# Fewer, larger transfers for the transposed keys of an attention kernel, and a list schedule that counts the issue time of the SP queue

## The chip, the cores and the metric

The kernel runs on one core of a Trainium2 chip. It is written in a Python kernel language that gives each engine its own instruction stream: PE (TensorE: matrix products and transposes), DVE (VectorE), ACT (ScalarE), POOL (GpSimd) and SP (SyncE, whose queue issues nearly all DMA transfers). The engines run at the same time and each works through its own stream in order; they wait for one another through semaphores. The metric is the device time of one launch in microseconds (us), lower is better.

## The reference

The program computes a recurrent attention over 768 steps for 4 batches of 8 heads (head dimension 40), and then a mixture of eight experts on its output.

```python
for t in range(S):                       # S=768; r,k,v,w,a,b are (4,8,768,40)
    y[:, :, t] = np.einsum('bhd,bhde->bhe', rt, state)
    Sa = np.einsum('bhde,bhe->bhd', state, at)
    state_decay = state * wt[:, :, None, :] - np.einsum('bhd,bhe->bhde', Sa, bt)
    state = state_decay + np.einsum('bhd,bhe->bhde', vt, kt)
...
xc = x[x @ w_skip > 0]                   # x: y as (3072, 320)
e_idx = np.argmax(xc @ w_gate, axis=1)   # one of 8 experts a row
h = np.maximum(xc[mask] @ w1[e], 0.0)    # (320,1024)
y[mask] = gate_w[mask, None] * (h @ w2[e])
out[do_compute] = xc + y
```

## The kernel before

**Tiling.** The 768 steps are cut into 24 chunks of 32 steps. All 32 combinations of batch and head go through a chunk together; they stand in two halves, x=0 and x=1, of 16 units each. Two consecutive chunks 2h and 2h+1 share their loaded inputs and everything that is worked out from these, and such a set (the code's index `h`, 0 to 11) is called a pair here; the change's title calls it a head pair. Per chunk and half the kernel makes small matrix products on PE: `rs` (state times r), `ux`, `uq` (with the inverse of a triangular matrix), `sst` (the state for the next chunk) and `yy` (the output). The left factors that hold the keys and b's of a pair, transposed so that time lies on the partitions, are the tiles `L2[x][h%2]`, all parts of one buffer `L2t`; two pairs' worth of them exist. `sst` and `yy` read them.

**How L2 is filled.** `kbt(h,bb)` (line 395) transposes a quarter of the 16 units of pair h: four PE transposes into one PSUM bank (`pt`), then ACT copies. It is called four times for each pair, bb=0 to 3, in chunk 2h-1, one chunk ahead of the pair. Four parts of the bank (two chunks by two halves) go to different partitions or columns of L2. For pair 0 ACT writes them there directly, in four copies of 64 partitions a quarter. For all other pairs one ACT copy takes the quarter into a staging piece of the buffer `SCR`, and four DMA transfers, issued by SP, carry the parts to L2. There are two staging pieces, at columns 1024 and 1536 of `SCR`, used in turn by the quarters (pair 1 has only the first). A copy into a piece can start only when the transfers have read what the same piece held. The first 1024 columns of `SCR` hold another thing, `VR`, which ACT writes and SP transfers to `R1t` (`load_v`).

**Order.** From chunk 1 to chunk 21 nothing is issued as written. The class `Rec` records every operation as a task, and `flush` hands them out in the order of a list schedule: `plan` simulates the five engines with the durations that `cost` gives and takes, step by step, the task that can start first, with priority by `key`. So each engine's order, SP's too, follows from `cost`'s numbers, and the line of all recorded instructions in a profile is 227 (`flush`); those issued as they are written have line 114 (`call`). `cost` returns for a DMA how long it holds its queue and how long it takes after that. Before the change it puts 0.06 us of holding on SP. PSUM banks for the products are assigned by the plan also (`pc`, `pq`, `ps` in the profile).

After chunk 23 come the experts, issued in written order.

Of the kernel before, what the change touches and what calls it, by code (L numbers as in the profile page):

```python
# [8 lines left out]
F32 = mybir.dt.float32  # L9
# [7 lines left out]
B,H,S,D=4,8,768,40  # L17
# [40 lines left out]
class Rec:  # L58
# [34 lines left out]
    def cost(s,e,op,w,r,a):  # L93
        sz=lambda x: int(np.prod([d[1] for d in list(x.ap)[1:]])) if len(list(x.ap))>1 else 1
        n=max(sz(x) for x in (w[:1]+r[:1]))
        if 'dma' in op:
            by=4*n*min(128,w[0].ap[0][1])
            if 'ind' in op:
                s.ni+=1; return (3.6 if s.ni%2 else 1.05),2.6
            return (0.06 if e=='S' else 0.6),2.2+by/1.7e5  # L100
        if e=='P':
            if op=='transpose': return 0.145,0
            o=sz(w[0]); m,k=w[0].ap[0][1],r[0].ap[0][1]
            return (0.03+0.0006*o if m==40 else 0.04 if k<128 and o<70 else 0.0575 if k<128 else 0.03+0.00026*o),0
        if e=='A': return 0.15+0.00085*n,0
        if e=='G': return (0.08+n*0.0008 if op=='memset' else 0.18 if op=='tensor_copy' else 0.25+0.0021*n),0
        ps=any('PSUM' in str(x.space).upper() for x in w+r)
        if op=='tensor_tensor_scan': return 0.1+0.00217*n,0
        if op=='transpose': return 0.16+0.00115*n*(1 if n<1000 else 1.4),0
        if op=='memset': return 0.08+0.0003*n,0  # L110
        if op=='tensor_tensor': return 0.14+0.00105*n*(1 if ps else 1.6),0
        return 0.16+0.00105*n,0
# [147 lines left out]
def attn(ctx,tc,i,m,out,X):  # L260
# [4 lines left out]
    cp=P("const",1).pool; wk=P("wk",1); wk2=P("wk2",2); wk3=P("wk3",3); wk4=P("wk4",4)  # L265
# [5 lines left out]
    V,A,G,TE,SP=nc.vector,nc.scalar,nc.gpsimd,nc.tensor,nc.sync  # L271
# [13 lines left out]
    L1t=cp.tile([128,4096],F32,name="L1t")  # L285
    l1s=[[WR[:,8192:9216],WR[:,9216:10240],WR[:,10240:11264]]+[l3]+[L1t[:,1024*q:1024*q+1024] for q in range(4)]][0]
    L1=[[l1s[2*n+x].rearrange("p (u c t) -> p u c t",u=16,c=2) for n in range(NL)] for x in range(2)]
    TB=cp.tile([128,NTB*512],F32,name="TB"); SCR=cp.tile([128,2048],F32,name="SCR")
    TBa=[TB[:,512*q:512*q+512].rearrange("p (h m) -> p h m",h=16) for q in range(NTB)]
    L2t=cp.tile([128,5120],F32,name="L2t"); R1t=cp.tile([128,5632],F32,name="R1t")  # L290
    L2=[[L2t[:,1280*(2*n+x):1280*(2*n+x)+1280].rearrange("p (c u d) -> p c u d",c=2,u=16) for n in range(NL2)] for x in range(2)]
# [103 lines left out]
    def kbt(h,bb):  # L395
        if h>=NH: return
        KB=H[h]['KB']
        pt=ps_p.tile([128,4,128],F32,tag="pp",name="pt")
        for hh in range(4):
            u=bb*4+hh  # L400
            TE.transpose(pt[:,hh,:104],KB[0:PR,u].rearrange("p c k t -> p (c k t)"),idn[0:PR,0:PR])
        if h==0:
            for c in range(2):
                for x in range(2):
                    A.copy(L2[x][0][64-64*x:128-64*x,c,bb*4:bb*4+4,:],pt[64*c:64*c+64,:,64*x:64*x+40])
            return
        o=1024 if h==1 or bb%2==0 else 1536
        sg=SCR[:,o:o+320].rearrange("p (x h d) -> p x h d",x=2,h=4)
        A.copy(sg.rearrange("p x h d -> p h x d"),pt.rearrange("p h (x d) -> p h x d",x=2)[:,:,:,0:40])
        for c in range(2):  # L410
            for x in range(2):
                SP.dma_start(L2[x][h%NL2][64-64*x:128-64*x,c,bb*4:bb*4+4,:],sg[64*c:64*c+64,x])
    def wex(h,c):
        if h>=NH: return
        H[h]['WE',c]=wk.tile([128,4,4,32],F32,tag="WE",name="WE")
        A.copy(H[h]['WE',c].rearrange("p h b t -> p b h t")[0:PR],H[h]['Wx'][0:PR,:,c*32:c*32+32].rearrange("p (b h) t -> p b h t",b=4))
# [181 lines left out]
    if 1:  # L598

        with tc.manual_schedule(engines={ET.Pool}):  # L600
# [35 lines left out]
            for b in range(4): kbt(0,b); warm(BX[16+b])  # L636
# [66 lines left out]
        for c in range(NC):  # L703
# [19 lines left out]
            if j==1: wtt(2*ph+1,0); wex(2*ph+1,1); kbt(2*ph+1,0)  # L723
# [3 lines left out]
            if j==3: kbt(2*ph+2,0)  # L727
# [390 lines left out]
def build(tc,i,out):  # L1118
    with ExitStack() as ctx:
        cp=ctx.enter_context(tc.tile_pool(name="mcp",bufs=1))  # L1120
        m=Moe(ctx,tc,i,out,cp)
        m.base1=cp.tile([128,8],F32,name="base1")
        m.fi=cp.tile([1,3],I32,name="fi"); m.cw=cp.tile([128,24],F32,name="cw"); tc.nc.gpsimd.memset(m.cw,0.0)
        m.zc=cp.tile([128,1],F32,name="zc"); tc.nc.gpsimd.memset(m.zc,0.0)
        m.wc=cp.tile([128,1],F32,name="wc"); tc.nc.vector.memset(m.wc,-WMID)
        m.WR=cp.tile([128,11264],F32,name="WR"); m.raw=[m.WR[:,0:5632],m.WR[:,5632:11264]]
        P=lambda n,b,**k: tc.tile_pool(name=n,bufs=b,**k)
        with tc.manual_schedule(engines={ET.PE,ET.Activation,ET.DVE}), P("pp",1,space=PSUM) as m.pp, P("rt",1) as rt, P("xp",1) as xp:
            m.wk,m.xp=Static(rt,1),Static(xp,2)
            with ExitStack() as c2: attn(c2,tc,i,m,out,m.X)  # L1130
            with P("mw2",2) as wk2, P("mw",1) as wk, P("mw4",4) as wk4: m.experts(wk,wk2,wk4,m.pr)
        general(m,m.fi,{q:i['raw_'+q] for q in 'rkvwab'},m.X)
# [13 lines left out]
```

## Time and profile before

| | us |
|---|---|
| median of 3 runs | 677.64 |
| lowest and highest run | 669.96, 680.13 |
| the profiled execution | 679.06 |
| its span, from the first to the last instruction | 677.3 |

Busy time of the engines in the span: PE 527.9 us (78%), DVE 452.6 us (67%), ACT 347.4 us (51%), POOL 301.1 us (44%). The share of TensorE's clock that was granted is 0.849 on average. The recorded part, chunks 1 to 21, lies at about 81 to 496 us, and the experts begin at about 556 us.

How to read it: a busy share is an average over stages with different limits, so it says little by itself. A row of the view of waits says how long an engine sat idle in total before a kind of instruction, and what ended that idle time. A row of the timeline gives the start, the duration, the engine and line, what is written from what, the count, and in brackets the idle time just before. SP has no computing: its rows are the issuing of transfers, one after the other.

### The profile page before, as it was taken

The numbers are of one execution on the slowest core, as the hardware profiler recorded it, in microseconds if no ns is written. First come the engines' busy times: TensorE is split into PE (matmuls) and PEld (weight loads), VectorE is DVE, ScalarE is ACT, GpSimd is POOL, SyncE is SP. The second block draws the span as 40 slices with busy tenths as digits, with TensorE's granted clock in tenths as the row PEclk, the third lists the DMA queues.
The fourth block names the chain that finished last, engine by engine and source line by source line (L and its number), as shares of the span: only waits on it lengthen the run. The fifth ranks groups of instructions, "written<-read, shape, count | busy, mean of one in ns | idle before, by whom it ended". The sixth has DMA issues, their size and how long they took to land.

```text
span 677.3 us, 29160 instructions
## 1 busy us (share of the span) xinstructions
PE 527.9 (78%) x12532; PEld 443.5 (65%) x12532; DVE 452.6 (67%) x1163; ACT 347.4 (51%) x801; POOL 301.1 (44%) x225
## 2 busy tenths in 40 slices
PE   5777266877785877868878778687886789999996
PEld 2544155666664666757656567576765479999996
DVE  7998573976579583776757657475466344689881
ACT  5563344564755536556464647465754154444550
POOL 5482842443536534365461651212221144666661
PEclk9777775988888787787997898778987689999999
DMA  7662686436566383643746444546336686776310
GB/s 196 204 211 100 176 238 172 125 79 176 147 166 165 77 237 76 186 131 81 214 108 193 103 145 114 140 118 167 93 82 155 203 239 188 217 224 216 108 43 29
DMA packets 105445, 102.32 MB, mean 151 GB/s; under 512 B 59316, under 2 KB 92673, under 8 KB 103822
## 3 DMA queue, kind: packets, MB, share of 16 engines
q1 hardware_dynamic: 103390, 96.61, 51.2%
q0 software_dynamic: 1920, 3.79, 1.7%
q8 instruction: 100, 1.64, 1.0%
q14 instruction: 35, 0.29, 0.1%
HBM read 74.03 MB, written 17.08 MB: 135 GB/s over the span
## 4 chain that ended last, share of the span: by engine, by line
PE 32%; DMA 9%; DVE 7%; issue 5%; SPq 3%; ACT 3%; POOL 1%; POOLq 0%; ACTq 0%; DVEq 0%
PE pc L227 7%; PE pc L114 6%; PE ps L114 6%; PE px L114 5%; PE pq L227 4%; DMA L2t<-SCR 4%; SPq L227 3%; PE ps L227 3%; DMA xg<-XS,ix 3%; DVE M L227 2%; ACT R1t L227 2%; DVE R1t L227 1%; DMA R1t<-SCR 1%; DVE px L227 1%; PE pq L114 1%
## 5 line engine op out<-in xcount | busy, mean ns | idle before, releaser
L227 POOL TENSOR_TENSOR R1t<-R1t,mc 64x512 f32<-64x512 f32 x42 | 56.1, 1336 | 157.3 <-ACT R1t L227 119.3
L227 ACT COPY R1t<-pc 32x288 f32<-32x288 f32 (+2 forms) x146 | 62.2, 426 | 31.5 <-PE pc L227 27.0
L114 POOL TENSOR_TENSOR WL<-WR,WH 128x1280 fp32r<-128x1280 f32 (+1 forms) x21 | 57.7, 2775 | 13.3 <-ACT WH L114 13.2
L227 DVE TENSOR_TENSOR px<-px,M 128x168 f32<-128x168 f32 (+10 forms) x240 | 58.0, 268 | 2.0
L227 DVE TENSOR_TENSOR M<-M,px 128x168 f32<-128x168 f32 (+10 forms) x240 | 55.1, 256 | 2.1
L227 DVE TENSOR_TENSOR R1t<-pc,D 40x512 f32<-40x512 f32 (+1 forms) x42 | 25.3, 601 | 27.4 <-PE pc L227 22.2
L114 ACT CAST WH<-WR 128x1024 fp32r<-128x1024 f32 (+1 forms) x35 | 39.6, 1131 | 0.0
L227 PE MATMUL pc<-UX,TB 32*32 32x72 f32 (+1 forms) x896 | 28.0, 274 | 13.4 <-ACT SCR L227 6.4
L227 POOL DMA_INDIRECT xg<-XS,ix x20 | 25.4, 1272 | 26.0 <-DVE px L227 8.8
L227 POOL TENSOR_TENSOR WR<-WR,M 128x1024 f32<-128x1024 f32 x14 | 30.3, 2175 | 13.4 <-DMA WR<-kb 12.0
L114 POOL DMA_INDIRECT out<-ro,ti x16 | 15.7, 982 | 42.5 <-DVE ro L114 12.4
L227 DVE TENSOR_TENSOR_SCAN M<-M 128x1041 f32<-128x1041 f32 (+1 forms) x14 | 34.5, 2461 | 0.1
L227 PEld LDWEIGHTS pc<-UX,TB 32*32 32x32 f32 x896 | 21.3, 125 | 19.1 <-ACT SCR L227 7.2
L227 ACT COPY R1t<-pq 32x416 f32<-32x416 f32 (+2 forms) x56 | 25.3, 452 | 16.1 <-PE pq L227 14.6
L227 PE MATMUL py<-L2t,R1t 128*32 128x40 f32 x1344 | 24.3, 219 | 11.8 <-POOL R1t L227 8.8
L114 ACT ACTIVATE hH<-pc 128x512 fp32r<-128x512 f32 x21 | 12.6, 599 | 40.0 <-PE pc L114 40.0
L114 PE MATMUL pc<-xH,WH 128*128 128x256 f32 x126 | 32.5, 283 | 0.0
L114 DVE TENSOR_TENSOR WL<-WR,WH 128x1024 fp32r<-128x1024 f32 (+1 forms) x19 | 24.9, 1309 | 11.1 <-ACT WH L114 7.7
L114 DVE CAST ti<-xe 128x2 int32<-128x2 f32 x8 | 30.5, 3816 | 0.2
L227 PE MATMUL pc<-R1t,L2t 128*40 128x72 f32 (+1 forms) x560 | 24.7, 243 | 7.5 <-ACT R1t L227 2.4
L227 PEld LDWEIGHTS py<-L2t,R1t 128*32 128x32 f32 x1344 | 19.0, 123 | 16.8 <-POOL R1t L227 9.7
L227 ACT COPY SCR<-pc 128x320 f32<-128x320 f32 (+1 forms) x28 | 13.2, 472 | 32.1 <-DMA L2t<-SCR 28.4
(396 smaller groups left out, 1633.1 us busy)
## 6 DMA issues: line engine op xcount, KB each, us to landing
WR<-kb SPq DMA_DIRECT2D x10, 1024.0 KB
WR<-w SPq DMA_DIRECT2D x16, 640.0 KB
WR<-w SPq DMA_DIRECT2D x16, 512.0 KB
L2t<-SCR SPq DMA_DIRECT2D x176, 40.0 KB
vvt<-vv SPq DMA_DIRECT2D x12, 512.0 KB
rrt<-rr SPq DMA_DIRECT2D x12, 512.0 KB
M<-wt SPq DMA_DIRECT2D x9, 520.5 KB
M<-at SPq DMA_DIRECT2D x8, 512.0 KB
```

Source lines behind the costliest of these rows:

```text
L114: if not s.on: return fn(*a,**k)
L227: for fn,a,k,own in s.tasks[i].calls: (fn if s.en[i]==s.tasks[i].e else s.nc.vector.tensor_copy)(*[at(x,own) for x in a],**{n:at(x,own) fo ...
```

## The change

Three things change. First, a staging tile for a whole pair: `SCR` grows from 2048 to 2304 columns, its columns 1024 to 2303 hold all four quarters, and after the last quarter four transfers of 160 KB carry the pair, in place of 16 of 40 KB, four after each quarter. Second, pair 1 is treated as pair 0: ACT writes L2 directly, four copies a quarter, and there is no transfer. Third, in `cost`, a transfer holds SP's queue for 0.6 us in place of 0.06, and a product with 64 output partitions (those of `m2p`) is priced like one with 40.

```diff
@@ cost
-            return (0.06 if e=='S' else 0.6),2.2+by/1.7e5
+            return 0.6,2.2+by/1.7e5
...
-            return (0.03+0.0006*o if m==40 else 0.04 if k<128 and o<70 else 0.0575 if k<128 else 0.03+0.00026*o),0
+            return (0.03+0.0006*o if m in (40,64) else 0.04 if k<128 and o<70 else 0.0575 if k<128 else 0.03+0.00026*o),0
@@ attn
-    TB=cp.tile([128,NTB*512],F32,name="TB"); SCR=cp.tile([128,2048],F32,name="SCR")
+    TB=cp.tile([128,NTB*512],F32,name="TB"); SCR=cp.tile([128,2304],F32,name="SCR")
@@ kbt
-        if h==0:
+        if h<2:
             for c in range(2):
                 for x in range(2):
-                    A.copy(L2[x][0][64-64*x:128-64*x,c,bb*4:bb*4+4,:],pt[64*c:64*c+64,:,64*x:64*x+40])
+                    A.copy(L2[x][h][64-64*x:128-64*x,c,bb*4:bb*4+4,:],pt[64*c:64*c+64,:,64*x:64*x+40])
             return
-        o=1024 if h==1 or bb%2==0 else 1536
-        sg=SCR[:,o:o+320].rearrange("p (x h d) -> p x h d",x=2,h=4)
-        A.copy(sg.rearrange("p x h d -> p h x d"),pt.rearrange("p h (x d) -> p h x d",x=2)[:,:,:,0:40])
+        sg=SCR[:,1024:2304].rearrange("p (x u d) -> p x u d",x=2,u=16)
+        A.copy(sg[:,:,4*bb:4*bb+4].rearrange("p x u d -> p u x d"),pt.rearrange("p h (x d) -> p h x d",x=2)[:,:,:,0:40])
+        if bb<3: return
         for c in range(2):
             for x in range(2):
-                SP.dma_start(L2[x][h%NL2][64-64*x:128-64*x,c,bb*4:bb*4+4,:],sg[64*c:64*c+64,x])
+                SP.dma_start(L2[x][h%NL2][64-64*x:128-64*x,c],sg[64*c:64*c+64,x])
```

What this moves in the program's order is shown at three places; in these rows a name is a tile, written from others, and `x4` says that four alike follow each other.

On SP, pair 6 (the middle of the recorded part) reads before the change, beginning just behind the first quarter's four transfers to `L2t`:

```order
L227 DMA R1t<-SCR 32x8x64 x2
L227 DMA L2t<-SCR 64x160 x4
L227 DMA WR<-M 32x256 x4
L227 DMA M<-zer 32x1024
L227 DMA WR<-M 32x256 x4
L227 DMA vvt_149<-vv 128x1024
L227 DMA R1t<-SCR 32x8x64 x2
L227 DMA M<-at 128x1024
L227 DMA L2t<-SCR 64x160 x4
L227 DMA R1t<-vt 32x16x40
L227 DMA WR<-kb 128x2048
L227 DMA L2t<-SCR 64x160 x4
```

The same pair on SP with the change:

```order
L227 DMA R1t<-SCR 32x8x64 x2
L227 DMA WR<-M 32x256 x4
L227 DMA M<-zer 32x1024
L227 DMA R1t<-SCR 32x8x64 x2
L227 DMA vvt_149<-vv 128x1024
L227 DMA WR<-kb 128x2048
L227 DMA L2t<-SCR 64x640 x4
L227 DMA R1t<-vt 32x16x40
L227 DMA M<-at 128x1024
L227 DMA WR<-M 32x256 x4
```

Sixteen transfers have become four, all behind the load of the next keys (`WR<-kb`), and the others keep nearly their order.

On ACT, the staging copies of pair 6 (`SCR<-... 128x4x2x40`) from the second quarter on, before the change, with the semaphores that each instruction waits for (DMAHW are those of SP's transfers):

```order
L227 COPY SCR<-pq_99 128x4x2x40 [waits DMAHW2_49,DMAHW7_49,DMAHW1_49,PE_49]
L227 COPY R1t<-ps_103 32x288 [waits PE_49,Pool_49]
L227 COPY R1t<-ps_103 32x288 x3
L227 ACTIVATE ex_984<-sb_983 128x16 [waits DVE_49]
L227 COPY SCR<-pq_99 128x512 [waits DMAHW6_49,DMAHW5_49,PE_49]
L227 COPY SS_116<-pc_100 40x320 [waits PE_49]
L227 COPY SS_116<-pc_100 40x320
L227 COPY SCR<-ps_103 128x4x2x40 [waits DMAHW1_49,DMAHW2_49,DMAHW0_49,DMAHW7_49,PE_49,Activation_49]
L227 COPY R1t<-pc_100 32x288 [waits PE_49,Pool_49]
L227 COPY R1t<-pc_100 32x288 x3
L227 COPY SCR<-ps_103 128x4x2x40 [waits DMAHW5_49,DMAHW6_49,DMAHW0_49,DMAHW7_49,PE_49,Activation_49]
```

And with the change:

```order
L227 COPY SCR<-pc_101 128x4x2x40 [waits PE_49]
L227 COPY SCR<-pc_100 128x512 [waits DMAHW6_49,DMAHW5_49,PE_49]
L227 COPY UX_452<-pq_99 128x4x72 [waits PE_49]
L227 COPY SCR<-pc_101 128x4x2x40 [waits PE_49]
L227 COPY SS_116<-ps_103 40x320 [waits PE_49]
L227 COPY SS_116<-ps_103 40x320
L227 COPY SCR<-pc_101 128x4x2x40 [waits PE_49]
L227 COPY R1t<-pc_100 32x288 [waits PE_49,Pool_49]
L227 COPY R1t<-pc_100 32x288 x3
```

The second, third and fourth staging copy of a pair no longer wait for a transfer; the first still waits for those of the pair before.

On PE, pair 7: from the last transposes (`<-mc,WR 128x104 x4`) on, before the change. The first product that reads the new pair's `L2t` (`<-R1t,L2t 40x72 x8`) stands 16 rows behind this first row:

```order
L227 MATMUL pq_99<-mc,WR 128x104 x4
L227 MATMUL ps_102<-mc,WE_454 128x104 x4
L227 MATMUL pc_100<-UX_452,TB 32x72 x16
L227 MATMUL pq_99<-rrt_152,SS_116 40x64 x16
L227 MATMUL py_104<-L2t,R1t 32x40 x16
```

With the change, the rows at the end of the same distance, which is now 19 rows:

```order
L227 MATMUL py_104<-L2t,R1t 32x40 x16
L227 MATMUL pq_99<-wg,xT_980 32x9 x12
L227 MATMUL ps_103<-WR,L1t 32x64 x16
L227 MATMUL pq_99<-WR,L1t 32x64 x16
L227 MATMUL pc_101<-R1t,L2t 40x72 x8
```

The products that read a pair's keys stand about as far behind its transposes as they did.

## Rows read from the trace of the kernel before

**Rows 1.** The page: busy time of the engines.

```profile
PE 527.9 (78%) x12532; PEld 443.5 (65%) x12532; DVE 452.6 (67%) x1163; ACT 347.4 (51%) x801; POOL 301.1 (44%) x225
```

**Rows 2.** The chain of waits by engine and line, shares of the window, first of 200 to 300 us (of which the chain covers 263 to 300), then of 300 to 400, then of 400 to 510 us.

```profile
by line: DVE M L227 9.1%; PE pq L227 5.7%; DVE px L227 5.0%; DVE R1t L227 4.4%; PE pc L227 3.7%; PE ps L227 3.0%; POOL R1t L227 2.5%; issue 1.3%; PE py L227 0.8%; DVE XS L227 0.6%; DVE pos L227 0.4%; POOL D L227 0.4%; DVE base L227 0.2%; DV
...
by line: PE pc L227 16.6%; PE pq L227 12.1%; issue 11.9%; DMA L2t<-SCR 10.6%; ACT R1t L227 9.5%; SPq L227 9.0%; PE ps L227 7.7%; DVE R1t L227 5.1%; DVE M L227 4.1%; DVE px L227 2.0%; DMA R1t<-SCR 2.0%; ACT SCR L227 1.4%; ACT WE L227 1.4%; P
...
by line: PE pc L227 22.0%; DMA L2t<-SCR 13.1%; SPq L227 12.7%; PE pq L227 8.9%; PE ps L227 8.5%; issue 7.6%; DMA R1t<-SCR 6.0%; DVE WH L114 3.6%; DVE R1t L114 3.4%; ACT R1t L227 3.2%; DMA L1t<-zer 2.7%; PE py L227 1.9%; PE pc L114 1.5%; ACT
```

**Rows 3.** The chain of waits in order of time: links on the transfers from `SCR` to `L2t`, the shortest, one in the middle and the two longest of seven (start, length).

```profile
330.28 5.76 DMA L2t<-SCR
...
351.36 2.96 DMA L2t<-SCR
...
439.51 6.65 DMA L2t<-SCR
...
465.62 1.87 DMA L2t<-SCR
```

**Rows 4.** The view of one tile, `L2t`: the issuing of its transfers on SP (count, then shortest, median and longest in ns, first and last start in us).

```profile
L227 SPq DMA_DIRECT2D L2t<-SCR x176: 461/594/1884, 98.5 to 504.3; - x176
```

**Rows 5.** Waits of ACT and of PE between 95 and 505 us: who waited for what, us in total, times, longest.

```profile
ACT SCR L227 <- DMA L2t<-SCR: 38.4, 11, 5.9
...
PE pc L227 <- ACT SCR L227: 19.4, 7, 4.4
...
PE ps L227 <- ACT SCR L227: 3.6, 1, 3.6
...
PE pq L227 <- ACT SCR L227: 2.0, 3, 0.8
```

**Rows 6.** Timelines of PE from 95 to 515 us: the rows where PE had stood idle until a staging copy that itself had waited for a transfer, and the two where it had stood idle until a transfer to `L2t` landed.

```profile
103.50 0.96 PE L227 MATMUL pc<-mc,WR 104*128 104x104 f32 x4 [4.38 <-ACT SCR L227]
...
108.68 1.30 PE L227 MATMUL pc<-L2t,R1t 128*40 128x40 f32 x32 [1.71 <-ACT SCR L227]
...
114.86 1.19 PE L227 MATMUL pc<-UX,TB 32*32 32x72 f32 x32 [2.77 <-ACT SCR L227]
...
153.80 0.95 PE L227 MATMUL ps<-mc,WR 104*128 104x104 f32 x4 [3.58 <-ACT SCR L227]
...
193.08 1.18 PE L227 MATMUL pc<-UX,TB 32*32 32x72 f32 x32 [2.76 <-ACT SCR L227]
...
336.08 1.18 PE L227 MATMUL pc<-R1t,L2t 128*40 128x72 f32 x14 [1.91 <-DMA L2t<-SCR]
...
354.90 0.42 PE L227 MATMUL pc<-oh,mc 128*32 128x16 f32 x16 [3.62 <-ACT SCR L227]
...
358.91 1.94 PE L227 MATMUL pq<-rrt,SS 128*40 128x64 f32 x32 [0.76 <-ACT SCR L227]
...
446.29 1.15 PE L227 MATMUL ps<-R1t,L2t 128*40 128x72 f32 x14 [2.00 <-DMA L2t<-SCR]
...
468.08 1.09 PE L227 MATMUL pc<-rrt,SS 128*40 128x64 f32 x32 [3.30 <-ACT SCR L227]
```

**Rows 7.** Timelines of pair 6 at its fourth quarter: the staging copy on ACT, then the issuing on SP from there to the quarter's transfers.

```profile
318.62 0.43 ACT L227 COPY SCR<-ps 128x320 f32<-128x320 f32 x1 [0.78 <-ACT R1t L227]
...
319.68 2.41 SPq L227 DMA_DIRECT2D WR<-M  x4
...
325.36 3.45 SPq L227 DMA_DIRECT2D L2t<-SCR  x4
...
329.63 0.56 SPq L227 DMA_DIRECT2D WR<-kb  x1
330.28 3.59 SPq L227 DMA_DIRECT2D L2t<-SCR  x4
```

**Rows 8.** Timelines of pair 7: its fourth staging copy on ACT, that quarter's transfers on SP, and the first product on PE that reads the new pair's keys.

```profile
358.43 0.43 ACT L227 COPY SCR<-pq 128x320 f32<-128x320 f32 x1 [1.69 <-DMA L2t<-SCR]
...
365.33 2.71 SPq L227 DMA_DIRECT2D L2t<-SCR  x4
...
373.70 2.15 PE L227 MATMUL pc<-R1t,L2t 128*40 128x72 f32 x32 [1.60 <-ACT R1t L227]
```

**Rows 9.** Busy time by stretches: length, busy time (and instructions) of PE, PE's weight loads, DVE, ACT and POOL, then the granted clock, the share of DMA and GB/s.

```profile
250.00:300.00 50.00, 39.65 (x1084) 33.02 (x1084) 33.44 (x133) 28.34 (x71) 25.74 (x20) 0.76 0.53 146
300.00:350.00 50.00, 41.40 (x1201) 34.20 (x1203) 33.36 (x104) 28.32 (x72) 25.58 (x21) 0.83 0.49 137
350.00:400.00 50.00, 36.57 (x1180) 30.64 (x1178) 33.81 (x107) 27.11 (x70) 23.50 (x20) 0.83 0.49 136
```

**Rows 10.** Timelines: ACT's direct copies to `L2t` for the first two quarters of pair 0, one staging copy of 128x320 with its wait in pair 1, and one of `m2p`'s sets of 16 products on PE (each of them two passes).

```profile
25.93 2.39 ACT L114 COPY L2t<-px 64x160 f32<-64x160 f32 x8
...
103.02 0.43 ACT L227 COPY SCR<-pc 128x320 f32<-128x320 f32 x1 [5.77 <-DMA L2t<-SCR]
...
312.35 1.15 PE L227 MATMUL pq<-rrt,vvt 40*64 40x64 f32 x32
```

**Rows 11.** Waits from 95 to 125 us, in the chunk in which pair 1 is prepared.

```profile
ACT SCR L227 <- DMA L2t<-SCR: 10.7, 3, 5.8
...
PE pc L227 <- ACT SCR L227: 8.9, 3, 4.4
```

**Rows 12.** Waits of SP's own queue between 95 and 505 us.

```profile
SPq L227 <- PE pc L227: 35.7, 33, 5.0
```

## The prediction

> **What bounds the kernel now.** I read the page first: PE is busy for 78% of the span and DVE for 67%, so neither is a wall by itself and the time lies in how they wait for each other [rows 1]. The chain of waits says on what. It covers the time from 263 us, and the recorded part ends near 505. In its last two windows the reader is to see two names that do no arithmetic: the transfers from `SCR` to `L2t` hold 10.6% of 100 us and 13.1% of 110 us, and SP's own queue 9.0% and 12.7% [rows 2]. That is 25.0 us and 23.0 us. Before 300 us neither name stands among those listed, and there DVE's links (`M`, `px`, `R1t`) lead with 18.5% of 100 us [rows 2]. So the staging of the keys is on the path in some pairs and off it in others.
>
> Then the view of waits shows the mechanism. ACT sat idle 38.4 us, 11 times, before a staging copy that waited for a transfer [rows 5]: the third and fourth quarter of a pair need a piece that SP has not yet emptied. ACT works in order, so everything behind such a copy waits, and PE waits for ACT.
>
> Why is SP late? An issue takes 594 ns in the median, and 176 of them go to `L2t` [rows 4]. For pair 6 the fourth staging copy began at 318.62 and took 0.43 us, so it was done at 319.05. SP was issuing other things and reached its four transfers at 330.28, 11.2 us later [rows 7]. PE stood idle for 1.91 us until they landed, at 336.08 [rows 6].
>
> **The change, part by part.** The sums are made against the profiled execution, 679.06 us, which lies 1.4 us above the median of the three runs and inside their spread of 10 us. I make no correction for that.
>
> *Staging for a whole pair.* Each quarter has a place of its own, so the second to fourth copy wait for PE alone. The first waits for the transfers of the pair before, issued about two chunks earlier, which I cost at nothing: at worst it is the 5.8 us of the longest ACT wait seen [rows 11], once a pair. What goes is PE's idle time behind the waiting copies. I take only the PE rows whose copy itself had waited for a transfer: 4.38 + 1.71 + 2.77 + 3.58 + 2.76 + 3.62 + 0.76 + 3.30 = 22.9 us [rows 6]. The view's totals (19.4 + 3.6 + 2.0 = 25.0 us, rows with `VR`'s copies included) agree with it [rows 5].
>
> *4 transfers for 16.* 136 issues go: 12 for each of ten pairs and 16 of pair 1. At 0.594 us they are 80.8 us of SP's time between 98 and 505 us [rows 4], or 7.1 us a pair. What this is worth directly are the two stalls in which PE itself waited for a landing, 1.91 + 2.00 = 3.9 us [rows 6]. SP's other transfers come earlier too; I count nothing for that, and the chain's 23.0 us of SP is its upper bound [rows 2].
>
> Here one rule speaks against the change. The row says that an issue costs 0.594 us, against links of 1.87 to 6.65 us from issue to landing [rows 3, 4], and that it stands in line: 16 of them are 9.5 us a pair. The Trainium skill (DMA: Bandwidth & Descriptors, Issuing engines are not separate DMA queues) says that the time a sequencer takes to initiate a DMA is usually small relative to the DMA itself. By that rule the 3.9 us would not be won, and the sum below would end 3.2 us higher, at 660.5; the trace does not agree here, since short transfers one behind the other make a queue of 11.2 us [rows 7].
>
> *A transfer of 160 KB for 40 KB.* The trace has no such transfer from `SCR`. From below it lands as a 40 KB one does, 2.96 us after its issue; from above it takes the longest link, 6.65 us, which is one behind the 1 MB load of keys or a run of four [rows 3]. I take the upper value, and it is hidden: in pair 7 the fourth copy ended at 358.86 and PE read the new keys first at 373.70 [rows 8], so 14.8 us lie between; four issues (2.71 there, 3.59 in pair 6 [rows 7, 8]) and a landing of 6.65 need 10.2. What is left, 4.6 us, is what SP may be behind. The changed order on PE leaves about the same distance, 19 rows for 16. That all four quarters now go last costs nothing as long as this holds; if the cover goes, see the slower rival.
>
> *Pair 1 by direct copies.* ACT makes 16 copies of 0.299 us (2.39 / 8) for four of 0.426 [rows 10], so 4.8 for 1.7 us, 3.1 us more. Three ACT waits of together 10.7 us are gone in the same chunk [rows 11], and they hide it; without that cover it costs 3.1 us at most. The bank in PSUM is held three copies longer, 0.9 us, which lies behind other products. The 8.9 us of PE's idle time there [rows 11] are in the sum above.
>
> *The planner's two prices.* They issue nothing. 0.6 us agrees with the row, 0.594, and 0.068 us for a product of `m2p` is near the 1.15 / 16 = 0.072 measured, where it had 0.04 [rows 4, 10]. So the plan is made with truer numbers, and the order moves a little everywhere. From below that costs what a single new wait of PE costs, the longest seen being 4.38 us [rows 6]; from above it takes more of SP off the chain, up to the 23.0 us. I take nothing.
>
> *What is late next.* 22.9 + 3.9 = 26.8 us of stalls go. Not all of it is kept: from 250 to 350 us, where only 1.9 us of these stalls stand, PE is still idle for 10.4 and 8.6 of 50 us, 19%, while from 350 to 400 it is idle for 13.4 [rows 9]. So I let 19% of the freed time go idle again, behind DVE and POOL, and keep 0.81 x 26.8 = 21.7 us. The sum: 679.1 - 21.7 = 657.4, forecast 657 us.
>
> **The rivals.**
>
> *More: SP leaves the path.* If all `L2t` links of the chain after 300 us go (25.0) and the stalls before 300 (4.38 + 1.71 + 2.77 + 3.58 + 2.76 = 15.2), without a new wait in their place, it is 40.2 us, and 639 us. For it speaks that SP's relief reaches transfers that I counted at nothing; against it that a chain link removed bares the next-longest path.
>
> *Hidden: another path as long.* The 37 us of chain before 300 us hold DVE, not SP [rows 2], and the clean stretch is no faster in PE's work (its granted clock is 0.76, below the 0.83 of the stretches after it) [rows 9]. If DVE's and POOL's preparation paces the pairs, only pair 1's 8.9 us are won, where nothing is repeated: 670 us. Against it speaks the half of the chain that does name SP and `L2t`.
>
> *Slower: a whole pair behind SP's queue.* All four transfers now start after the fourth copy. If SP is as far behind there as it was in pair 6, 11.2 us, then 11.2 + 3.6 + 6.65 is 21.5 us against the 14.8 there are, and `sst` waits 6.7 us; with it everything behind it on PE. In ten pairs that is 67 us, the ACT term (0.81 x 22.9 = 18.5) is still won, and the time 679.1 - 18.5 + 67 = 728 us. It is slower than before from 1.9 us of lateness a pair (SP 6.5 us behind), by over 2% from 3.2. SP also waits itself, 35.7 us in 33 times for products on one bank alone, 5.0 at the longest [rows 12], and a transfer behind such a row is held. Against it: in the same stretch 12 issues, 7.1 us, are gone ahead of the transfers, so that 11.2 becomes about 4.1, inside the 4.6 that are spare. It is close, which is why it keeps a chance.
>
> That the planner undoes the change (late transfers kept, quarters issued apart) is excluded by the order: ten runs of four transfers, and copies that wait for PE alone.
>
> **How the numbers follow.** The forecast has a chance of 0.49; its own range is 645 to 668, from stalls that are kept whole with some of SP's relief to half of them. The more-rival has 0.16, the hidden one 0.25 (666 to 684), the slower one 0.10. About 2%, 13.6 us, is what a measurement of this kernel can tell from no change, so faster means below 664.1 us. That takes 0.44 of the forecast, all of the more-rival, and 0.01 of the hidden: 0.61. Within 2%: 0.05 of the forecast and 0.23 of the hidden, 0.28. Slower: the slower rival and a bad end of the hidden one, 0.11. For 8 in 10 the range leaves out the slower rival and half of the more-rival: 638 to 686.
>
> **What would show it.** In the changed profile, ACT's idle time before copies to `SCR` that ends with a transfer to `L2t` should fall from 38.4 us to under 8; PE's eight stalls behind them should be gone; 40 issues should stand for `L2t`; the chain should hold under 3% on each of `L2t`'s transfers and SP's queue where it held 10 to 13% and 9 to 13%. PE's first product on a new pair's keys should not wait for a transfer. I am wrong if PE stands idle for landings to `L2t` in most pairs (slower rival), or if those stalls go and the idle time comes back whole behind DVE, POOL or ACT's `R1t` copies (hidden).

## The result and the profile after

| | before | with the change |
|---|---|---|
| median of 4 runs, us | 674.71 | 644.61 |
| lowest and highest run, us | 669.96, 680.13 | 639.57, 650.5 |
| the profiled execution, us | 679.06 | 647.78 |
| its span, us | 677.3 | 646.0 |
| PE busy in the span, us | 527.9 | 512.4 |
| PE idle in the span (span less busy), us | 149.4 | 133.6 |
| granted TensorE clock, mean of the span | 0.849 | 0.884 |

The changed kernel takes 0.9553 of the time before, with an interval of 0.9442 to 0.9663: 4.5% faster, 30 us. It ran once more in a later series, where it took 641.48 us, 0.9496 of before [0.9443, 0.9549]. The forecast was 657 us with a range of 638 to 686; the time lies in that range, 0.4 us under the forecast's own 645 to 668, and nearer to the more-rival's 639 than to 657. Medians are of all runs, while every ratio, and the clocks in the table of the experiments, leave out runs that took over 1.5% more than the fastest of the same kernel.

The page of the changed kernel gives the line that answers to [rows 1]:

```profile
PE 512.4 (79%) x12532; PEld 426.4 (66%) x12532; DVE 447.1 (69%) x1161; ACT 349.5 (54%) x815; POOL 299.7 (46%) x225
```

PE does the same 12532 products in 15.5 us less busy time, and its idle time is 15.8 us shorter. The two halves of the gain are about equal, and only the second is of the kind that the forecast summed.

The view of the tile `L2t`, against [rows 4], shows the issues, and then ACT's direct copies for pair 1 (against [rows 10]):

```profile
L227 SPq DMA_DIRECT2D L2t<-SCR x40: 462/594/1700, 150.7 to 464.1; - x40
...
L227 ACT COPY L2t<-pc x16: 284/287/290, 95.4 to 104.8; 64x160 f32<-64x160 f32 x16
```

There are 40 issues for 176, and a transfer of four times the size costs the same 594 ns on SP. In the view of waits from 80 to 505 us ACT has no row any more in which a copy to `SCR` waits for a transfer to `L2t` (38.4 us in [rows 5]), and PE waits for staging copies in these two rows alone (25.0 us in [rows 5]; in each row the us in total, the times, the longest):

```profile
PE pq L227 <- ACT SCR L227: 1.0, 3, 0.4
...
PE pc L227 <- ACT SCR L227: 0.5, 1, 0.5
```

PE has no row for a landing to `L2t` at all. Pair 6 shows why. These are ACT's row of its fourth staging copy, then SP's rows from there, then PE's first product on the new keys, from three timelines (against [rows 7] and, for the first read, [rows 8]):

```profile
296.64 0.43 ACT L227 COPY SCR<-pc 128x320 f32<-128x320 f32 x1 [0.26 <-PE pc L227]
...
296.93 1.43 SPq L227 DMA_DIRECT2D WR<-kb  x1
298.45 3.65 SPq L227 DMA_DIRECT2D L2t<-SCR  x4
...
304.25 5.09 SPq L227 DMA_DIRECT2D WR<-M  x4
...
318.65 0.70 PE L227 MATMUL ps<-R1t,L2t 128*40 128x72 f32 x16
```

The copy ends at 297.07 and SP starts the transfers at 298.45, 1.4 us later, where it had been 11.2 us behind before the change. The product at 318.65 has no bracket, so PE had not stood idle before it.

One view speaks against the easy reading. This is the chain of waits by line, of 200 to 300, 300 to 400 and 400 to 480 us, against [rows 2]:

```profile
by line: PE pc L227 20.8%; DMA L2t<-SCR 18.1%; PE pq L227 14.6%; DVE M L227 11.2%; ACT R1t L227 9.2%; PE ps L227 5.6%; DVE px L227 5.6%; DVE R1t L227 4.6%; issue 4.0%; DMA L1t<-M 3.5%; ACT SCR L227 2.4%; PE py L227 1.6%; SPq L227 1.4%; POOL
...
by line: PE pc L227 25.2%; PE ps L227 10.7%; DMA L2t<-SCR 9.8%; PE pq L227 9.6%; issue 9.0%; ACT R1t L227 8.7%; DMA R1t<-vt 5.9%; SPq L227 4.9%; DMA WR<-M 4.0%; DMA L1t<-M 3.7%; ACT SCR L227 3.2%; DVE R1t L227 2.4%; DVE M L227 1.1%; ACT WE 
...
by line: PE pc L227 21.2%; issue 16.3%; PE pq L227 10.0%; ACT R1t L227 9.3%; PE pc L114 7.6%; PE ps L227 6.8%; DMA WR<-w 4.9%; DVE R1t L227 3.7%; ACT SCR L227 3.6%; DMA R1t<-SCR 2.3%; PE pq L114 2.2%; PE py L227 2.0%; PE ps L114 2.0%; DVE R
```

SP's queue fell from 9.0% and 12.7% to 1.4%, 4.9% and no place among the names listed, but transfers to `L2t` still stand at 18.1% and 9.8%. In order of time these are two long links, the second followed by a transfer of another tile:

```profile
225.16 8.31 DMA L2t<-SCR
233.53 0.61 SPq L227
...
299.03 9.75 DMA L2t<-SCR
308.80 3.97 DMA WR<-M
```

The link that starts at 299.03 crosses the border of the two windows, and both count it whole. So `L2t` holds 18.1 us of the 200 us from 200 to 400, which is 9.0%, and not 27.9 us.

Nobody reads the keys at the end of these links: what waited was SP itself. In the program's order every transfer on SP waits for the semaphore that the one eight places earlier used, so a transfer that is slow to land holds the eighth behind it; in pair 6 the four `WR<-M` from 304.25 on took 5.09 us to issue, the last of them behind the landing at 308.78. From that landing the chain goes by `WR<-M` (to 312.77) and DVE to a product of PE at 315.04. SP's own waits from 80 to 475 us show such rows:

```profile
SPq L227 <- DMA WR<-kb: 12.4, 6, 2.7
...
SPq L227 <- DMA L2t<-SCR: 3.5, 4, 1.5
```

Whether these links cost anything is asked in the experiments below.

Last, the windows (columns as in [rows 9]) from 300 to 450 us:

```profile
300.00:350.00 50.00, 36.05 (x1207) 29.88 (x1199) 37.72 (x126) 27.35 (x70) 22.01 (x16) 0.89 0.72 186
350.00:400.00 50.00, 41.20 (x1337) 34.10 (x1333) 29.89 (x116) 31.33 (x79) 22.33 (x21) 0.90 0.46 118
400.00:450.00 50.00, 42.98 (x1415) 35.56 (x1419) 35.01 (x123) 31.48 (x80) 12.56 (x11) 0.97 0.60 156
```

From 350 to 400 us PE does 1337 products where it did 1180, at a granted clock of 0.90 where it had 0.83. The higher clock goes with the other half of the gain, the shorter busy time.

### The profile page after: what moved, and what is told of

It is laid out like the page before. It is cut to its first block, busy times and chain, and to the rows that moved or that the text cites. A ratio compares the mean times of both kernels' runs of the same rounds, so it can differ in the third digit from the quotient of the medians.

```text
span 646.0 us, 28910 instructions
## 1 busy us (share of the span) xinstructions
PE 512.4 (79%) x12532; PEld 426.4 (66%) x12532; DVE 447.1 (69%) x1161; ACT 349.5 (54%) x815; POOL 299.7 (46%) x225
## 4 chain that ended last, share of the span: by engine, by line
PE 44%; issue 12%; ACT 12%; DVE 11%; DMA 11%; POOL 3%; SPq 1%; POOLq 0%; ACTq 0%; DVEq 0%
PE pc L227 13%; PE pq L227 7%; ACT R1t L227 6%; PE ps L114 6%; PE pc L114 6%; PE ps L227 5%; PE px L114 5%; DMA L2t<-SCR 3%; DMA xg<-XS,ix 3%; DVE M L227 3%; DVE M L114 2%; DMA xe<-xg 2%; DVE R1t L227 2%; ACT SCR L227 1%; DVE px L227 1%
## 5 line engine op out<-in xcount | busy, mean ns | idle before, releaser
L227 ACT COPY R1t<-pc 32x416 f32<-32x416 f32 (+2 forms) x150 | 65.5, 437 | 38.0 <-PE pc L227 33.6
L227 DVE TENSOR_TENSOR R1t<-pc,D 40x512 f32<-40x512 f32 (+1 forms) x44 | 26.7, 606 | 21.8 <-PE pc L227 18.3
L114 POOL DMA_INDIRECT out<-ro,ti x16 | 15.7, 981 | 44.5 <-DVE ro L114 12.4
L227 ACT COPY R1t<-pq 32x288 f32<-32x288 f32 (+2 forms) x65 | 27.5, 423 | 12.5 <-PE pq L227 8.2
L227 PE MATMUL pc<-UX,TB 32*32 32x104 f32 (+1 forms) x928 | 27.4, 260 | 6.8 <-issue 3.5
L114 DVE CAST ti<-xe 128x2 int32<-128x2 f32 x8 | 31.9, 3982 | 0.2
L227 PE MATMUL ps<-R1t,L2t 128*40 128x40 f32 (+1 forms) x608 | 24.5, 229 | 8.0 <-issue 7.3
L227 PEld LDWEIGHTS py<-L2t,R1t 128*32 128x32 f32 x1344 | 18.0, 119 | 16.7 <-issue 12.4
L114 PE MATMUL ps<-WH,hH 128*128 128x320 f32 x88 | 28.6, 325 | 0.0
L114 PE MATMUL ps<-mc 128*128 128x512 f32 x34 | 24.4, 830 | 4.8 <-DMA mc<-mc 3.3
```

Source lines behind the costliest of these rows:

```text
L114: if not s.on: return fn(*a,**k)
L227: for fn,a,k,own in s.tasks[i].calls: (fn if s.en[i]==s.tasks[i].e else s.nc.vector.tensor_copy)(*[at(x,own) for x in a],**{n:at(x,own) fo ...
```

## The experiments

Two explanations were tried against each other: the **waits** (each quarter has its own place, so ACT and PE no longer stall) and the **issues** (136 fewer entries on SP, so everything SP carries comes earlier). The planner's prices and pair 1's direct copies were tried apart. All ratios are to the kernel before on the same chip.

| kernel | issues to `L2t`, and added ones | median us | ratio | PE idle us | clock, mean of its runs behind the ratio |
|---|---|---|---|---|---|
| before | 176 | 677 | 1 | 149.4 | 0.847 to 0.850 |
| e1, prices only | 176 | 665.38 | 0.9824 [0.9784, 0.9865] | 149.5 | 0.864 |
| e3, whole tile, 16 transfers a pair | 160 | 664.8 | 0.9823 [0.9781, 0.9865] | 145.5 | 0.874 |
| e5, whole tile alone, 16 transfers | 176 | 660.64 | 0.9732 [0.968, 0.9785] | 144.8 | 0.873 |
| e8, the change and 120 tiny transfers | 40 + 120 | 667.0 | 0.9852 [0.9804, 0.99] | 145.2 | 0.871 |
| e2, old prices | 40 | 645.77 | 0.9494 [0.9433, 0.9556] | 130.8 | 0.883 |
| e4, pair 1 staged | 44 | 650.26 | 0.9586 [0.9527, 0.9644] | 124.7 | 0.865 |
| e7 and f3, keys loaded after | 40 | 644.18, 642.22 | 0.9319 [0.9254, 0.9384], 0.9446 [0.9369, 0.9524] | 127.3, 125.6 | 0.890, 0.890 |
| e6 and f2, all pairs direct | 0 | 635.65, 638.42 | 0.9368 [0.9325, 0.9411], 0.942 [0.9359, 0.9481] | 124.0, 128.6 | 0.889, 0.889 |
| f1, all direct, old prices | 0 | 641.02 | 0.9483 [0.9431, 0.9535] | 125.7 | 0.882 |
| c_after, the change again | 40 | 641.48 | 0.9496 [0.9443, 0.9549] | 127.0 | 0.884 |

PE's idle time is the span less PE's busy time in each kernel's profiled execution, which need not lie near the median: e5's took 668.22 us and e6's 646.53, the longest of their runs, and e3's 657.55, the shortest. The medians of before in the three series were 676.86, 677.77 and 677.13 us. The column of the idle time divides the kernels cleanly: all five with 160 or 176 issues have 144.8 to 149.5 us (mean 146.9), all those with at most 44 have 124.0 to 133.6 (mean 127.5, with the first profile of the change), whatever their waits and prices.

**The two prices alone (e1).** The kernel before, with:

```diff
-            return (0.06 if e=='S' else 0.6),2.2+by/1.7e5
+            return 0.6,2.2+by/1.7e5
...
-m==40
+m in (40,64)
```

> The kernel before with the planner's two new prices alone: 176 transfers of 40 KB, two staging pieces, as before. If the gain of 30 us is the staging waits (first theory), the prices give little: 668 to 678 us, and ACT still waits over 30 us for transfers to L2t before its staging copies. If the gain is SP's issuing as the planner sees it (rival), the plan alone wins most of it: 645 to 655 us. If it is the number of issues on SP (second rival), 670 to 690, since a plan that knows of a queue that is too long can only spread the lateness.

It gained 1.8%, 12 us, and lies in none of the three ranges. The stalls are larger than before. Waits of ACT, then of PE, from 80 to 505 us:

```profile
ACT SCR L227 <- DMA L2t<-SCR: 43.9, 16, 7.0
...
PE ps L227 <- ACT SCR L227: 18.2, 7, 6.7
...
PE pc L227 <- ACT SCR L227: 7.7, 8, 1.7
...
PE pq L227 <- ACT SCR L227: 5.8, 5, 2.1
```

PE waits 31.7 us for staging copies where it was 25.0 [rows 5], and its whole idle time is as before, 149.5. What fell is its busy time, 527.9 to 514.7. So a plan with truer prices did not avoid the stalls; other waits became shorter by as much, and the products ran at a higher clock, 0.868 in the profiled execution against 0.849.

**The tiles without the prices (e2).** The change, with both prices put back.

> The changed kernel with the planner's two old prices: the whole-pair tile, 4 transfers, direct copies for pairs 0 and 1. First theory (waits gone) and second rival (issues gone) both expect most of the gain here: 645 to 655 us. If the plan's prices are the cause: 665 to 677 us.

It takes 0.9494, the change itself 0.9496 and 0.9553. On top of the tiles the prices are worth nothing that can be measured, although alone they gave 1.8%. The parts do not add.

**The whole tile with 16 transfers (e3).** The change, but each quarter is sent when it is copied:

```diff
-        if bb<3: return
...
-                SP.dma_start(L2[x][h%NL2][64-64*x:128-64*x,c],sg[64*c:64*c+64,x])
+                SP.dma_start(L2[x][h%NL2][64-64*x:128-64*x,c,bb*4:bb*4+4,:],sg[64*c:64*c+64,x,4*bb:4*bb+4])
```

> The changed kernel with 16 transfers of 40 KB a pair from the whole-pair tile, each four issued after their quarter; new prices, pair 1 direct. The staging waits are away, 120 more issues are on SP than in the changed kernel (71 us of its time). First theory (waits): 645 to 652 us, as the change. Second rival (number of issues): 660 to 675 us, most of the gain lost.

ACT no longer waits for any transfer to `L2t`, pair 1 is direct, the prices are new, and yet the time is that of e1, 0.9823 against 0.9824: with the new prices, taking these waits away won nothing. PE itself now waits 7.4 us for landings to `L2t`. By the middle values e3 is even slower than e5 below (0.9823 against 0.9732, the intervals only just overlap), so the new prices did not help a kernel with 16 transfers a pair from the whole tile. The chain by line of this kernel, 300 to 400 us and then 400 to 480:

```profile
by line: SPq L227 29.8%; PE pc L227 10.7%; ACT R1t L227 7.4%; DMA WR<-kb 6.4%; PE pq L227 6.1%; issue 6.0%; DMA out<-XS 4.7%; DMA L1t<-zer 4.3%; PE ps L227 3.8%; DMA WR<-M 3.8%; DVE M L227 3.7%; DVE px L227 2.6%; DMA L1t<-M 2.6%; DMA R1t<-v
...
by line: SPq L227 18.1%; PE pc L227 15.7%; PE pq L227 9.7%; PE ps L227 9.0%; ACT R1t L227 7.9%; DMA L2t<-SCR 7.7%; issue 7.0%; DMA R1t<-SCR 6.3%; DMA R1t<-vt 5.8%; DVE R1t L227 5.1%; PE pc L114 2.2%; ACT SCR L227 1.6%; DVE px L227 1.1%; PE 
```

SP's queue is now the first name in both windows, where the change has it at 4.9% and not among the names listed.

**The whole tile alone (e5).** The kernel before with the tile of e3, pair 1 staged, old prices.

> The kernel before with the whole-pair staging tile alone: four transfers of 40 KB after each quarter (176 in all), pair 1 staged, old prices. The staging waits go, nothing else. First theory (waits): 650 to 660 us. Number of issues (after the first runs the likelier): 668 to 682 us, no gain beyond a few us, with PE's idle time behind staging copies gone and SP's queue on the chain.

It gained 2.7%, 18 us, and at 660.64 us lies between the two ranges, at the edge of the first. Its transfers, from the view of `L2t`, and then PE's waits from 80 to 505 us:

```profile
L227 SPq DMA_DIRECT2D L2t<-SCR x176: 462/594/1996, 102.3 to 491.6; - x176
```

```profile
PE pc L227 <- DMA L2t<-SCR: 8.2, 1, 8.2
...
PE ps L227 <- DMA L2t<-SCR: 7.6, 2, 5.4
PE pq L227 <- DMA L2t<-SCR: 7.3, 2, 4.1
```

The stalls behind staging copies have gone to 1.3 us, and 23.1 us of waiting for the landings have come in their place. The stall was moved from the copy, which waited for SP's earlier transfers, to the product, which waits for its later ones. In the profiled execution PE's idle time fell by 4.6 us only, its busy time by 6.4; that execution is 7.6 us above the median, so it shows 11 of the 18 us.

**The change with the issues put back (e8).** After each of the first three quarters of ten pairs four transfers of 64 x 2 numbers (512 bytes) go from the staging tile to a tile that nobody reads; nothing of the kernel's result depends on them.

```diff
-        if bb<3: return
+        if bb<3:
+            for q in range(4): SP.dma_start(DUM[0:64,2*(4*bb+q):2*(4*bb+q)+2],sg[64*(q%2):64*(q%2)+64,q//2,4*bb,0:2])
+            return
```

> The changed kernel with 12 more transfers a pair on SP, of 8 bytes in each of 64 partitions, out of the staging tile into a tile that nothing reads (120 issues in all, about 71 us of SP's time). No wait of ACT or PE hangs on them and they move next to nothing. If issue time on SP is the cause: 655 to 672 us. If it is the small transfers' landing or the staging waits: 642 to 650 us, as the change.

```profile
L227 SPq DMA_DIRECT2D DUM<-SCR x120: 461/594/1965, 139.7 to 485.5; - x120
```

This row of the tile `DUM` shows that a transfer that moves next to nothing costs SP the same 594 ns. With 120 of them the kernel takes 0.9852 where the change takes 0.9496 and 0.9553: 0.030 to 0.036 of 677 us, 20 to 24 us, are given back, and PE's idle time is 145.2 again. The staging is as in the change, with 40 transfers of 160 KB, so this loss comes from the 120 entries themselves. How it reaches PE shows in part in PE's waits from 80 to 505 us, where the change has no such row:

```profile
PE ps L114 <- DMA L2t<-SCR: 4.3, 1, 4.3
...
PE ps L227 <- DMA L2t<-SCR: 2.9, 2, 2.2
...
PE pc L227 <- DMA L2t<-SCR: 2.6, 1, 2.6
```

So the transfers that carry keys land too late there, and PE stands idle 9.8 us for them. One thing in the expectation is not so: the first staging copy of the next pair does have to wait for the added transfers, as it writes over what they read. But no idle time of ACT in the profile ends with one. The profile puts 22.9 us of idle time of DVE and POOL down to them, in three waits before work that reads and writes other tiles; what ended these is not known. Whether the loss is their 71 us of SP's time (120 x 0.594) or the places that they take among the eight semaphores was not told apart.

**Pair 1 staged (e4).** The change with `if h<1` in place of `if h<2`.

> The changed kernel with pair 1 staged and carried by four transfers, as the others. By the sum of the prediction pair 1 held 8.9 us of PE's stalls, which the whole-pair tile removes just as well, so direct copies should be worth little: 642 to 650 us. If pair 1's direct copies are what wins there (the staging tile must wait for nothing, but the transfers go behind a full SP queue at the start), 650 to 656 us.

0.9586 against 0.9494 (e2, same series), 0.9496 and 0.9553: 2 to 6 us by the middle values, and the intervals overlap. The median, 650.26 us, lies at the border of the two ranges and decides for neither. In this kernel too no copy to `SCR` waits for a transfer to `L2t` between 80 and 135 us: the whole tile by itself removes pair 1's stalls, and the direct copies add at most a little.

**All pairs direct (e6, f2, f1).** No staging and no transfers: ACT writes all parts of L2, 16 copies a pair; f2 is e6 again, f1 has the old prices.

```diff
-        if h<2:
-            for c in range(2):
...
+        for c in range(2):
+            for x in range(2):
+                A.copy(L2[x][h%NL2][64-64*x:128-64*x,c,bb*4:bb*4+4,:],pt[64*c:64*c+64,:,64*x:64*x+40])
```

> The changed kernel with direct ACT copies for all pairs, as pairs 0 and 1 have them, and no transfer to L2t. If an issue is worth what the change shows (30 us / 136 = 0.22 us each), 40 fewer give 9 us, 636 us; against it stand 3.1 us more of ACT's time a pair, 31 us in all. 632 to 645 us if SP still matters and ACT has room, 648 to 665 if ACT (54% busy) now paces the pairs.

> Direct ACT copies for all pairs with the new prices, once more, beside the changed kernel. If the 40 issues still left cost as the others did (16 to 22 us for 120 to 136, so some 5 us) and the 8 to 10 us landings of the 160 KB transfers hold SP up: 630 to 638 us, 5 to 10 us under the changed kernel. If ACT's extra 31 us eat that: 640 to 646.

> Direct ACT copies for all pairs with the planner's two old prices. If the plan only needs to know of SP's issue time while SP is crowded, the prices are worth nothing here: 632 to 640 us, as with the new ones. If they order the rest better in any kernel: 642 to 650 us.

ACT is busy for 377.4 us in e6 where it was 349.5 with the change, and PE waits for these copies for little: 1.1 us in e6, 3.0 in f2 and 2.9 in f1. e6 with 0.9368 lies below both measurements of the change, its repeat with 0.942 [0.9359, 0.9481] overlaps them, and so does f1 with 0.9483. The medians of f2 and f1, 638.42 and 641.02, fall between the ranges of their expectations and decide for neither. So this is the fastest version in the medians and certainly faster than before; against the change it is between equal and 2% faster. The last 40 issues are worth 13 us by the widest pair of middle values (0.9553 less 0.9368), and may be worth nothing.

**The load of keys behind the transfers (e7, f3).** The planner is told to place each 1 MB load of keys (`WR<-kb`), which stands ahead of the pair's four transfers in SP's order, behind them. This takes away what the long links of 8.31 and 9.75 us stood behind.

```diff
+        t.late=s.hold if s.kb else ()
...
+            for j in t.late: t.p.add(j)
```

> The changed kernel with the planner told that a load of the next keys (1 MB) comes after the four transfers of the pair, which it stood ahead of. The profile of the change has transfers to L2t on the chain that take 8.3 and 9.8 us. If the 1 MB load ahead of them makes them late and this is on the path: 630 to 640 us. If that lateness is hidden by the 14.8 us there are: 641 to 650 us, no change that can be told.

> The load of the next keys behind the pair's transfers, once more, beside the changed kernel. The first look had runs from 629 to 648 us, so it did not tell. If the late landings behind the 1 MB load matter: 630 to 638 us; if not: 640 to 648.

In e7 pair 6's four transfers start at 297.50 and the load behind them at 304.62. e7's six runs lie between 628.57 and 647.57 us, too far apart to tell, so its ratio is not used. In f3 the median is 642.22 against 641.48 for the change in the same series, and the intervals overlap. Did the edit take away what it was meant to? The chains can't say: those of e7, f3 and c_after, the change's own second profile, reach back to 357, 352 and 352 us only, and in what they cover e7 has one link on `L2t` (4.18 us, at 465.95), the others none. But SP's rows say so. These are pair 6's four `WR<-M` in c_after, the same in f3, and f3's row of SP's waits for the load from 80 to 475 us:

```profile
298.85 7.09 SPq L227 DMA_DIRECT2D WR<-M  x4
...
299.28 2.46 SPq L229 DMA_DIRECT2D WR<-M  x4
...
SPq L229 <- DMA WR<-kb: 0.7, 2, 0.5
```

With the order turned round SP's waits for the load fall from 12.4 us (14.5 in c_after) to 3.2 in e7 and 0.7 in f3, its row for `L2t` is gone in both, and the four `WR<-M` are issued without a hold. So this hold-up of SP was taken away, and the time did not change by anything that can be measured.

**The change again (c_after).**

> The changed kernel itself, beside the three others on the same chip: 640 to 648 us by every theory.

It gives 0.9496; the two measurements of the change overlap. Its profiled execution has 127.0 us of idle time where the first had 133.6, so two profiles of one kernel differ by 6.6 us there, a third of the 19.4 us between the two groups.

## Why the forecast was right, and where its terms were not

*Direction and mechanism.* The forecast said that two things go, ACT's and PE's stalls behind copies and SP's lateness, and that what remains hides the new transfers. In the changed kernel that is so: no staging copy waits for a transfer, not even a pair's first, whose wait was priced at nothing (its worst case, 5.8 us, misread the longest wait, 5.9 in [rows 5]); PE's eight stalls [rows 6] are gone, 40 issues stand for `L2t`, and no product of PE waits for a landing to `L2t`. Of its marks in the profile one failed: the chain was to hold under 3% on `L2t`'s transfers and on SP's queue. It holds 9.0% on the former from 200 to 400 us and up to 4.9% on the latter. What each of the two things is worth, the forecast had wrong, as the next three points show. That the time still lies in the range is in part luck, for the terms were off in opposite directions: the idle time won was less than forecast, and the shorter busy time had no term.

*The step that was mis-sized* is "SP's other transfers come earlier too; I count nothing for that". The forecast gave the missing issues 3.9 us, 3.2 kept. Put back (e8) they cost 20 to 24 us, and from e5 to e2 (the same tile, 4 transfers for 16, pair 1 direct, the old prices in both) the ratio goes from 0.9732 to 0.9494, 16 us. That is close to the upper bound that the forecast named and set aside, the chain's 23.0 us of SP.

*The ACT term* (22.9 us, 18.5 kept) has the right size for the wrong reason. e5 has only this part, and gained 18 us; but in its profile PE waited 23.1 us for landings in place of 22.9 for copies. With the new prices the same step won nothing (e1 to e3). So it is not a sum that can be put beside the issues' term; as long as 16 transfers stand in the queue, the stall finds another place. The forecast's total for idle time, 21.7 us, came out as 15.8 and 22.4 in the two profiles of the change.

*Busy time taken as fixed.* The sum counted idle time alone. PE's busy time went from 527.9 to 512.4 and 512.7 us with the same products, at a clock of 0.884 for 0.849. This is not peculiar to the change: e1, with no idle time won, has 514.7, and there it is the whole gain. It goes with the clock, which in the table is 0.847 to 0.850 before and 0.864 to 0.890 in every other kernel. Of the 31.3 us between the two profiled executions 15.5 are of this kind, and no term stood for them; of idle time 15.8 us came where 21.7 were forecast. Together that is 9.6 us more than the sum; the other 3.2 us to the median of 644.6 are the distance of the profiled execution from it. The 16 to 24 us of the issues are the same gain sorted by cause, and not to be added to this.

*The rule that spoke against the change.* The row here was 594 ns an issue, and the forecast kept to it. e8 decides for counting the entries, by a wider margin than was assumed: 120 of them cost 20 to 24 us in all. The Trainium skill (DMA: Bandwidth & Descriptors, Issuing engines are not separate DMA queues) says that initiating a DMA is usually small relative to the DMA itself. For one transfer the rows agree, 0.594 us against links of 1.87 to 6.65 us; for many in one queue the forecast's reading of it, that nothing would be won, is not what was measured.

*The transfer of 160 KB.* It was given 6.65 us as an upper value; two took 8.31 and 9.75. The cover held even so, since SP came sooner than assumed: 1.4 us behind the copy in pair 6, where the forecast had 4.1. The one on the chain landed at 308.78, 9.9 us before the first read.

*Pair 1.* 8.9 us of stalls went [rows 11]. They are gone with pair 1 staged in the whole tile as well (e4), and in the changed kernel 5.4 us of PE's idle time between 95 and 125 us, before other products, end in "issue". The 16 copies took 0.287 us each, against 0.299 assumed.

*The prices* were taken at nothing, and beside the tiles that is right (e2). On the kernel before they are worth 1.8%.

*The rivals.* The more-rival came nearest: 639 us, by SP leaving the path. Its mechanism is half true: SP's queue all but left the chain, `L2t`'s links stayed in that of the first profile, up to 309 us, and the time fell all the same. The hidden rival, with pair 1's stalls alone won and 670 us, fell: 30 us were won, and e8 gives most of them back with pair 1 as the change has it. The slower rival fell with SP's lateness: 1.4 us in pair 6 where it needed 6.5.

*What stays open.* PE's idle time that ends in "issue", for which the profile shows no wait, rose from 22.5 to 42.8 us, so more than half of the 36.1 us that left the waits with a known end came back there; no run here tells why. The link from a shorter queue on SP to a higher clock on PE was not tried by itself, and the total of idle time does not set the clock: e1 and e4 have nearly the same mean, 0.864 and 0.865, with 149.5 and 124.7 us of idle time. Last, every kernel here is planned anew, so some us of each difference may be the new order and not the part that was changed; the prices, which change only the plan, moved the time by 12 us in e1 and not at all beside the tiles.

## What to carry to other kernels

Count the entries of a DMA queue at their measured issue time before counting bytes: here 120 entries more were worth 3% at a volume that hardly changed, and four times the bytes per entry took no more issue time. Removing a wait in front of a full queue can move the stall to the next reader, as in e5, so give the queue fewer entries first and look at the stall again. Do not price a name in the chain of waits by its share: the load ahead of transfers that held 18.1 us of 200 could be moved behind them without an effect on the time that shows, while the entries of a queue that held 9 to 13% were worth more than half of what was won.

## What the runs showed of the hardware

An issue on SP took 594 ns in the median for 512 bytes (e8), 40 KB (before) and 160 KB (the change) alike, and 0.46 to 2.0 us singly.

At the places shown here the granted clock fell where PE had stood idle. These are windows of 10 us of the changed kernel, then three of PE's rows in them:

```profile
300.00:310.00 10.00, 5.79 (x238) 4.67 (x228) 5.27 (x8) 2.58 (x8) 5.30 (x4) 1.00 0.88 234
310.00:320.00 10.00, 6.56 (x149) 5.16 (x151) 6.94 (x22) 3.90 (x11) 6.23 (x5) 0.66 0.63 154
320.00:330.00 10.00, 9.40 (x322) 7.83 (x322) 6.96 (x40) 9.31 (x24) 4.23 (x4) 1.00 0.45 110
```

```profile
313.27 0.90 PE L227 MATMUL pq<-mc,XS 128*128 128x128 f32 x3 [4.11 <-DVE M L227]
...
315.04 1.61 PE L227 MATMUL pc<-UX,TB 32*32 32x104 f32 x32 [0.18 <-DVE M L227]
...
320.42 0.92 PE L227 MATMUL pc<-UX,TB 32*32 32x104 f32 x32
```

From 300 to 310 us the clock was at its upper level, 2.4 GHz, and PE idle for 4.21 of the 10 us. In the next 10 us, with a stall of 4.11 us, the mean is 0.66, so for about two thirds of them it was at the lower level, 1.2 GHz (1 - 0.66 = 0.34, over the 0.5 between the levels), and 32 products behind the stall took 1.61 us. From 320 us on, with PE busy again, it is back at 2.4 GHz, and 32 products of the same form took 0.92.

Behind a staging copy the same is seen in the kernel before. At 358.91, after stalls of 3.62 and 0.76 us, 32 products took 1.94 us [rows 6]; 32 products of the same form took, with no such stall just before,

```profile
366.19 1.09 PE L227 MATMUL pq<-rrt,SS 128*40 128x64 f32 x32
```

Products of this form also took 1.09 us at 468.08, straight behind a stall of 3.30 us [rows 6], so the very next product need not be slow. In the places shown, idle time of PE was paid for twice: once as such, and once in the products behind it. That fits the two halves of the gain; that it explains them was not tried by itself, and e1's clock rose with no less idle time.
